# Routing for two heads in one matmul, and score operands padded to 128 rows

## The chip, the cores and the metric

One core of a Trainium2 chip runs the whole program. The metric is device time in microseconds for one launch; runs of the kernel before lie between 767.99 and 769.62 us, with a median of 769.47 us over five. The program alternates between five engines that run side by side, each in the order of its own queue: TensorE (matmuls and transposes), VectorE, ScalarE, GpSimd (called POOL in the profile) and SyncE, which only issues DMAs here.

## The reference

Attention with clusters, then a gated feed-forward layer. There are 4 batches, 8 heads, 768 tokens, 64 dimensions per head and 16 clusters per head. Cut to what matters:

```python
q_assign = argmax(q_n @ c_n.T, axis=-1)        # nearest of 16 centroids, per head
k_assign = argmax(k_n @ c_n.T, axis=-1)
mask   = q_assign[:, None] == k_assign[None, :]
scores = where(mask, q @ k.T / sqrt(64), -1e9)
attn   = softmax(scores)
x      = (attn @ v), heads side by side         # [3072, 512]
out    = (sigmoid(x @ w_gate) * (x @ w_val)) @ w_out   # 512 -> 1536 -> 512
```

The length of a q or k row doesn't change which centroid is the largest, so the kernel normalizes only the centroids.

## The kernel before

The kernel is written with a tile framework that sets the semaphores, hands out the buffers of its pools and fixes the order of each engine's instructions before the run; program order gives the priority, and on the chip each engine works strictly in that fixed order.

The mask is not applied as a mask. For each token a one-hot vector of its cluster is appended below the 64 rows of q and k. The q rows are scaled by 1/8 and their one-hot by 240 (`COH`); the exponential of line 202 has a bias of -240. Where the clusters are equal, 240 is added and taken away again; where they differ, the exponential of about -240 is zero. The augmented operands `q_aug` and `k_aug` have 80 rows (64 + 16), 768 columns, fp16.

The work of one head has three parts.

- Part A, lines 110 to 146: SyncE loads q and k side by side into `qk`, GpSimd loads v into `vv` and appends a column of ones (lines 123, 127). In two halves of 384 tokens, TensorE transposes three 128x128 blocks into `t1` (line 138); ScalarE writes the scaled q into `q_aug` (141), k into `k_aug` (144) and k in float32 into `kT32` (146); VectorE writes q in float32 into `qT32` (145).
- Part B, `phaseB`, lines 147 to 184: for each half of 384 tokens and for q and k apart, a float32 matmul with the head's centroids (64 rows, 16 weight columns) gives 16 scores per token in PSUM (`clq`, line 152; `clk`, line 171; one PSUM buffer each). In the trace each of these routing matmuls is two instructions, called a group below. ScalarE copies the scores to SBUF (160, 179), GpSimd takes the maximum over the 16 partitions (`partition_all_reduce`, 162 and 181), and VectorE compares scores and maximum, which gives the one-hot vectors. For k the comparison writes straight into `k_aug` (184); for q it writes `qoh` (166), and ScalarE scales that by 240 into `q_aug` (167).
- Part C, `phaseC`, lines 186 to 219: in two blocks of 384 queries, for each of six chunks of 128 keys a score matmul `sc` (194), the exponential `es` on ScalarE (202) and an output matmul into `av` (203), 64 rows plus the row of sums from the ones. Then VectorE takes the reciprocal of the sums (211), GpSimd broadcasts it (213) and VectorE multiplies into `xT` (214). `sc` and `av` have two PSUM buffers each, `es` three.

Per batch, part A is written for all eight heads, then B and C with C two heads behind B (lines 221 to 225). The pools keep nine heads of augmented operands and of `qT32` and `kT32`; the small tiles of part B have three buffers for each name. After the fourth batch comes the feed-forward layer (lines 227 to 273) with 128x128 weights and 512 columns per matmul.

Of the kernel before, what the change touches and what calls it, by code (L numbers as in the profile page):

```python
# [8 lines left out]
FP = mybir.dt.float32  # L9
FPR = mybir.dt.float32r  # L10
BF = mybir.dt.bfloat16
HP = mybir.dt.float16
AF = mybir.ActivationFunctionType
ALU = mybir.AluOpType
# [4 lines left out]
def kernel(  # L19
# [11 lines left out]
    nc = tc.nc  # L31
    B, H, S, D = q.shape
    NCL = centroids.shape[1]
# [3 lines left out]
    QB = 384  # L37
    NQB = S // QB
    COH = 240.0
    scale = 1.0 / (D ** 0.5)  # L40

    const = ctx.enter_context(tc.tile_pool(name="const", bufs=1))
    xpool = ctx.enter_context(tc.tile_pool(name="xT", bufs=1))
# [23 lines left out]
        out=wo, in_=moe_w_out.rearrange("(fc p) m -> p fc m", p=128)  # L67
    )

    cT = const.tile([64, H, NCL], FP)  # L70
    with tc.tile_pool(name="cprep", bufs=2) as cp, tc.tile_pool(
        name="cpsum", bufs=2, space=bass.MemoryType.PSUM
    ) as cps:
        for h in range(H):
            cn = cp.tile([NCL, D], FP)
            nc.sync.dma_start(out=cn, in_=centroids[h])
            sq = cp.tile([NCL, D], FP)
            nc.scalar.activation(sq, cn, AF.Square, accum_out=None)
            ss = cp.tile([NCL, 1], FP)
            nc.vector.tensor_reduce(ss, sq, AX.X, ALU.add)  # L80
            nrm = cp.tile([NCL, 1], FP)
            nc.scalar.activation(nrm, ss, AF.Sqrt)
            rn = cp.tile([NCL, 1], FP)
            nc.vector.reciprocal(rn, nrm)
            cnn = cp.tile([NCL, D], FP)
            nc.vector.tensor_scalar(cnn, cn, rn, None, ALU.mult)
            tps = cps.tile([64, NCL], FP)
            nc.tensor.transpose(tps, cnn, ident[:NCL, :NCL])
            nc.scalar.copy(cT[:, h, :], tps)

    with tc.tile_pool(name="qkv", bufs=3) as qkvp, tc.tile_pool(
        name="vvp", bufs=9
    ) as vvp, tc.tile_pool(
        name="aug", bufs=9
    ) as augp, tc.tile_pool(name="esb", bufs=3) as esbp, tc.tile_pool(
        name="p_t1", bufs=2, space=bass.MemoryType.PSUM
    ) as p_t1, tc.tile_pool(
        name="p_cl", bufs=1, space=bass.MemoryType.PSUM
    ) as p_cl, tc.tile_pool(
        name="p_sc", bufs=2, space=bass.MemoryType.PSUM  # L100
    ) as p_sc, tc.tile_pool(
        name="p_av", bufs=2, space=bass.MemoryType.PSUM
    ) as p_av, tc.tile_pool(
        name="small", bufs=3
    ) as smallp, tc.tile_pool(
        name="qt32", bufs=9
    ) as qtp:
        for b in range(B):
            augs = {}
            for h in range(H):  # L110
                dc = h // 2
                r0 = (h % 2) * 64
                qk = qkvp.tile([128, NCH, 2, 64], FP)
                vv = vvp.tile([128, NCH, 65], HP)
                nc.sync.dma_start(
                    out=qk[:, :, 0, :],
                    in_=q[b, h].rearrange("(c p) d -> p c d", p=128),
                )
                nc.sync.dma_start(
                    out=qk[:, :, 1, :],  # L120
                    in_=k[b, h].rearrange("(c p) d -> p c d", p=128),
                )
                nc.gpsimd.dma_start(
                    out=vv[:, :, 0:64],
                    in_=v[b, h].rearrange("(c p) d -> p c d", p=128),
                )
                nc.gpsimd.tensor_copy(vv[:, :, 64:65].rearrange("p c x -> p (c x)"), ones6[:, :NCH])

                q_aug = augp.tile([80, S], HP)
                k_aug = augp.tile([80, S], HP)  # L130
                qT32 = qtp.tile([64, S], FP)
                kT32 = qtp.tile([64, S], FP)
                augs[h] = (q_aug, k_aug, vv, qT32, kT32)

                for g in range(2):
                    t1 = p_t1.tile([128, 3, 128], FP)
                    for cc in range(3):
                        nc.tensor.transpose(t1[:, cc, :], qk[:, g * 3 + cc, :, :], ident)  # L138
                    cols = bass.ts(g, 384)
                    t1f = t1.rearrange("p c x -> p (c x)")  # L140
                    nc.scalar.activation(
                        q_aug[0:64, cols], t1f[0:64, :], AF.Copy, scale=scale
                    )
                    nc.scalar.copy(k_aug[0:64, cols], t1f[64:128, :])  # L144
                    nc.vector.tensor_copy(qT32[:, cols], t1f[0:64, :])  # L145
                    nc.scalar.copy(kT32[:, cols], t1f[64:128, :])  # L146
            def phaseB(h):
                q_aug, k_aug, vv, qT32, kT32 = augs[h]
                for blk in range(2):
                    cols = bass.ts(blk, 384)  # L150
                    clq = p_cl.tile([16, 384], FP)
                    nc.tensor.matmul(  # L152
                        out=clq,
                        lhsT=cT[:, h, :],
                        rhs=qT32[:, cols],
                        start=True,
                        stop=True,
                    )
                    clqs = smallp.tile([16, 384], FP)
                    nc.scalar.copy(clqs, clq)  # L160
                    amq = smallp.tile([16, 384], FP)
                    nc.gpsimd.partition_all_reduce(  # L162
                        amq, clqs, 16, bass_isa.ReduceOp.max
                    )
                    qoh = smallp.tile([16, 384], HP)
                    nc.vector.tensor_tensor(qoh, clqs, amq, ALU.is_equal)  # L166
                    nc.scalar.activation(
                        q_aug[64:80, cols], qoh, AF.Copy, scale=COH
                    )
                    clk = p_cl.tile([16, 384], FP)  # L170
                    nc.tensor.matmul(  # L171
                        out=clk,
                        lhsT=cT[:, h, :],
                        rhs=kT32[:, cols],
                        start=True,
                        stop=True,
                    )
                    clks = smallp.tile([16, 384], FP)
                    nc.scalar.copy(clks, clk)  # L179
                    amk = smallp.tile([16, 384], FP)  # L180
                    nc.gpsimd.partition_all_reduce(  # L181
                        amk, clks, 16, bass_isa.ReduceOp.max
                    )
                    nc.vector.tensor_tensor(k_aug[64:80, cols], clks, amk, ALU.is_equal)  # L184

            def phaseC(h):
                dc = h // 2
                r0 = (h % 2) * 64
                q_aug, k_aug, vv, qT32, kT32 = augs[h]
                for qb in range(NQB):  # L190
                    av = p_av.tile([65, QB], FP)
                    for j in range(NCH):
                        sc = p_sc.tile([128, QB], FP)
                        nc.tensor.matmul(  # L194
                            out=sc,
                            lhsT=k_aug[:, bass.ts(j, 128)],
                            rhs=q_aug[:, bass.ts(qb, QB)],
                            start=True,
                            stop=True,
                        )  # L200
                        es = esbp.tile([128, QB], HP)
                        nc.scalar.activation(es, sc, AF.Exp, bias=nbias)  # L202
                        nc.tensor.matmul(  # L203
                            out=av,
                            lhsT=vv[:, j, :],
                            rhs=es,
                            start=(j == 0),
                            stop=(j == NCH - 1),
                        )
                    rden = smallp.tile([1, QB], FP)  # L210
                    nc.vector.reciprocal(rden, av[64:65, :])  # L211
                    rinv = smallp.tile([64, QB], FP)
                    nc.gpsimd.partition_broadcast(rinv, rden)  # L213
                    nc.vector.tensor_tensor(  # L214
                        xT[r0 : r0 + 64, dc, bass.ds(b * S + qb * QB, QB)],
                        av[0:64, :],
                        rinv,
                        ALU.mult,
                    )

            for i in range(H + 2):
                if i < H:
                    phaseB(i)
                if i >= 2:
                    phaseC(i - 2)

# [2 lines left out]
    if True:  # L229
        with tc.tile_pool(name="h", bufs=2) as hp, tc.tile_pool(  # L230
            name="gs", bufs=3
# [72 lines left out]
```

## Time and profile before

| | |
|---|---|
| median of 5 runs (range) | 769.47 us (767.99 to 769.62) |
| the profiled execution: its time, its span | 767.99 us, 766.2 us |
| TensorE matmuls, busy | 676.0 us, 88% of the span, 2088 instructions |
| TensorE weight loads, beside them | 235.3 us, 31% |
| ScalarE | 451.8 us, 59%, 892 instructions |
| VectorE | 377.2 us, 49%, 416 instructions |
| GpSimd | 265.8 us, 35%, 267 instructions |
| routing matmuls, lines 152 and 171 | 92.1 and 92.4 us busy, 128 instructions each |
| mean granted TensorE clock | 0.759 of full |

Busy times are sums over the whole span, in which the attention and the feed-forward layer have different limits. Matmuls overlap each other, and their ends are modelled, so their rate is read from one start to the next. A releaser behind an arrow is what ended the idle time ahead of an instruction.

### The profile page before, as it was taken

How to read it: one execution, taken by the hardware profiler on the slowest of the kernel's cores; microseconds unless marked ns; L12 is line 12 of the kernel's file. 1: busy time of each engine (PE TensorE's matmuls, PEld its weight loads, DVE VectorE, ACT ScalarE, POOL GpSimd, SP SyncE). 2: the span in 40 equal slices, each digit the busy share in tenths (PEclk: the TensorE clock that was granted, in tenths of full speed). 3: DMA queues.
4: the chain of work that ended last, by engine and by line, in shares of the span. 5: the costliest groups of instructions: out<-in, count | busy, mean ns of one | idle time of the engine just before them, and what ended most of it. 6: DMA issues, size and time to landing. Idle time of an engine off the chain costs nothing.

```text
span 766.2 us, 6830 instructions
## 1 busy us (share of the span) xinstructions
PE 676.0 (88%) x2088; PEld 235.3 (31%) x2088; DVE 377.2 (49%) x416; ACT 451.8 (59%) x892; POOL 265.8 (35%) x267
## 2 busy tenths in 40 slices
PE   0197999897799998789998788999889999999998
PEld 0032222242222223222222321222334444444443
DVE  1144565667446666745666674656755132131221
ACT  2188666788766678776667877666763233232232
POOL 4144555526455542554654255455210000000000
PEclk9999999987555557755555755555559999999999
DMA  7984100124210013230010310000000101101011
GB/s 127 186 125 99 10 5 6 10 28 71 62 26 6 5 10 53 46 83 6 6 11 6 51 42 0 0 1 1 0 1 0 56 3 53 41 15 56 15 41 55
DMA packets 81620, 27.21 MB, mean 36 GB/s; under 512 B 75952, under 2 KB 77488, under 8 KB 81584
## 3 DMA queue, kind: packets, MB, share of 16 engines
q1 hardware_dynamic: 53888, 18.91, 10.1%
q0 software_dynamic: 27696, 7.87, 10.0%
q8 instruction: 16, 0.26, 0.1%
q14 instruction: 20, 0.16, 0.1%
HBM read 28.34 MB, written 6.29 MB: 45 GB/s over the span
## 4 chain that ended last, share of the span: by engine, by line
PE 70%; ACT 12%; issue 8%; POOL 5%; DVE 2%; DMA 2%; ACTq 0%; SPq 0%; POOLq 0%; DVEq 0%
PE av L203 13%; PE sc L194 10%; PE clq L152 10%; PE clk L171 10%; PE gp L241 8%; PE vp L249 8%; PE op L262 8%; ACT es L202 8%; PE t L138 3%; POOL amq L162 2%; POOL amk L181 2%; DMA cn<-in_centroids_dram 1%; ACT k_aug L144 1%; DMA qk<-in_k_dram 1%; ACT kT L146 1%
## 5 line engine op out<-in xcount | busy, mean ns | idle before, releaser
L202 ACT ACTIVATE es<-sc,nbias 128x384 f16<-128x384 f32 x384 | 216.8, 578 | 119.1 <-PE sc L194 104.7
L203 PE MATMUL av<-es,vv 128*65 128x384 f16 x384 | 183.0, 485 | 28.1 <-ACT es L202 12.2
L211 DVE RECIPROCAL rden<-av 1x384 f32<-1x384 f32 x64 | 163.3, 2552 | 56.3 <-PE av L203 55.6
L194 PE MATMUL sc<-q_aug,k_aug 80*128 80x384 f16 x384 | 188.0, 499 | 1.9 <-ACT es L202 0.8
L162 POOL PARTITION_ALL_REDUCE amq<-clqs x64 | 92.4, 1443 | 121.8 <-ACT clqs L160 110.2
L203 PEld LDWEIGHTS <-vv 128*65 128x65 f16 x384 | 58.7, 156 | 170.0 <-issue 152.0
L258 DVE TENSOR_TENSOR hT<-g,vp 128x512 f16<-128x512 f32 x72 | 49.4, 687 | 124.8 <-PE vp L249 124.4
L181 POOL PARTITION_ALL_REDUCE amk<-clks x64 | 100.2, 1566 | 18.3 <-DVE qT L145 8.4
L171 PE MATMUL clk<-kT,cT 64*16 64x384 f32 x128 | 92.4, 823 | 5.0 <-ACT clks L179 5.0
L152 PE MATMUL clq<-qT,cT 64*16 64x384 f32 x128 | 92.1, 821 | 1.8 <-DVE qT L145 1.1
L257 ACT ACTIVATE g<-gp 128x512 f32<-128x512 f32 x72 | 43.0, 597 | 74.8 <-PE gp L241 74.8
L184 DVE TENSOR_TENSOR k_aug<-clks,amk 16x384 f16<-16x384 f32 x64 | 47.5, 742 | 58.5 <-POOL amk L181 58.1
L138 PE MATMUL t<-ident,qk 128*128 128x128 f32 x192 | 54.0, 415 | 23.8 <-ACT kT L146 14.1
L241 PE MATMUL gp<-xT,wg 128*128 128x512 f16 x288 | 74.8, 382 | 0.0
L249 PE MATMUL vp<-xT,wv 128*128 128x512 f16 x288 | 74.3, 381 | 0.0
L194 PEld LDWEIGHTS <-k_aug 80*128 80x128 f16 x384 | 49.9, 130 | 79.1 <-issue 60.8
L213 POOL PARTITION_BROADCAST rinv<-rden x64 | 43.6, 682 | 63.5 <-DVE rden L211 63.5
L166 DVE TENSOR_TENSOR qoh<-clqs,amq 16x384 f16<-16x384 f32 x64 | 43.7, 684 | 43.0 <-POOL amq L162 42.9
L262 PE MATMUL op<-wo,hT 128*128 128x512 f16 x288 | 63.1, 379 | 0.0
L145 DVE COPY qT<-t 64x384 f32<-64x384 f32 x64 | 34.8, 548 | 44.8 <-ACT k_aug L144 43.6
L138 PEld LDWEIGHTS t<-ident,qk 128*128 128x128 f32 x192 | 33.5, 208 | 65.4 <-ACT kT L146 41.7
L214 DVE TENSOR_TENSOR xT<-av,rinv 64x384 f16<-64x384 f32 x64 | 35.2, 550 | 25.9 <-POOL rinv L213 24.7
(37 smaller groups left out, 355.4 us busy)
## 6 DMA issues: line engine op xcount, KB each, us to landing
qk<-in_q_dram SPq DMA_DIRECT2D x32, 192.0 KB, 2.9
qk<-in_k_dram SPq DMA_DIRECT2D x32, 192.0 KB, 3.1
out_dram<-osb SPq DMA_DIRECT2D x24, 256.0 KB, 2.0
vv<-in_v_dram POOLq DMA_DIRECT2D x32, 96.0 KB, 3.5
wg<-in_moe_w_gate_dram POOLq DMA_DIRECT2D x1, 1536.0 KB, 10.8
wv<-in_moe_w_val_dram POOLq DMA_DIRECT2D x1, 1536.0 KB, 10.9
wo<-in_moe_w_out_dram POOLq DMA_DIRECT2D x1, 1536.0 KB, 18.2
cn<-in_centroids_dram SPq DMA_DIRECT2D x8, 4.0 KB, 5.0
```

The costliest lines, as they stand in the source:

```text
L138: nc.tensor.transpose(t1[:, cc, :], qk[:, g * 3 + cc, :, :], ident)
L152: nc.tensor.matmul(out=clq, lhsT=cT[:, h, :], rhs=qT32[:, cols], start=True, stop=True,)
L162: nc.gpsimd.partition_all_reduce(amq, clqs, 16, bass_isa.ReduceOp.max)
L171: nc.tensor.matmul(out=clk, lhsT=cT[:, h, :], rhs=kT32[:, cols], start=True, stop=True,)
L181: nc.gpsimd.partition_all_reduce(amk, clks, 16, bass_isa.ReduceOp.max)
L194: nc.tensor.matmul(out=sc, lhsT=k_aug[:, bass.ts(j, 128)], rhs=q_aug[:, bass.ts(qb, QB)], start=True, stop=True,)
L202: nc.scalar.activation(es, sc, AF.Exp, bias=nbias)
L203: nc.tensor.matmul(out=av, lhsT=vv[:, j, :], rhs=es, start=(j == 0), stop=(j == NCH - 1),)
L211: nc.vector.reciprocal(rden, av[64:65, :])
L241: nc.tensor.matmul(out=gp, lhsT=wg[:, dcc, fc, :], rhs=xT[:, dcc, bass.ts(t, TB)], start=(dcc == 0), stop=(dcc == NDC - 1),)
L249: nc.tensor.matmul(out=vp, lhsT=wv[:, dcc, fc, :], rhs=xT[:, dcc, bass.ts(t, TB)], start=(dcc == 0), stop=(dcc == NDC - 1),)
L262: nc.tensor.matmul(out=op, lhsT=hT[:, fc, bass.ts(tb, 128)], rhs=wo[:, fc, :], start=(fc == 0), stop=(fc == NFC - 1),)
```

## The change

- Routing (part B) works on pairs of heads. Centroids of an even head stand in rows 0 to 63 and columns 0 to 15 of a 128x64 weight, those of the odd head in rows 64 to 127 and columns 32 to 47; the rest is zero. The float32 q and k of two heads stand above each other in one tile `qkT` of 128 rows. One float32 matmul gives the scores of both heads at output partitions 0 to 15 and 32 to 47 of one PSUM tile `cl` (one buffer, for q and k in turn). ScalarE copies the two halves apart; maximum and comparison stay per head.
- The pair's part B stands ahead of the even head's turn in the loop, every second step.
- The scaling moves: q is scaled by 1/128, k by 1/15, the exponential by 240 (1/128 x 1/15 x 240 = 1/8). Both one-hot vectors are then plain ones, the q comparison writes straight into `q_aug`, and the ScalarE instruction of line 167 is gone.
- The augmented operands have 128 rows. Nine pairs of buffers are made once, with rows 64 to 127 set to zero (VectorE for q, GpSimd for k), and are used in turn. The pool of float32 operands has five pair tiles instead of nine single ones of each kind.

```diff
+    ks = 16.0 / COH
+    scale = 1.0 / (16.0 * D ** 0.5)
+    cTp = const.tile([128, H // 2, 64], FP)
+    nc.gpsimd.memset(cTp, 0.0)
...
-            nc.scalar.copy(cT[:, h, :], tps)
+            if h % 2 == 0:
+                nc.scalar.copy(cTp[0:64, h // 2, 0:NCL], tps)
+            else:
+                nc.scalar.copy(cTp[64:128, h // 2, 32 : 32 + NCL], tps)
...
+        for n in range(9):
+            qa_n = augp.tile([128, S], HP, tag=f"qa{n}")
+            ka_n = augp.tile([128, S], HP, tag=f"ka{n}")
+            nc.vector.memset(qa_n[64:128, :], 0.0)
+            nc.gpsimd.memset(ka_n[64:128, :], 0.0)
+            aug_bufs.append((qa_n, ka_n))
...
+                q_aug, k_aug = aug_bufs[(b * H + h) % 9]
+                if h % 2 == 0:
+                    qkT = qtp.tile([128, 2, S], FP)
+                    pairT[h // 2] = qkT
...
-                    nc.scalar.copy(k_aug[0:64, cols], t1f[64:128, :])
-                    nc.vector.tensor_copy(qT32[:, cols], t1f[0:64, :])
-                    nc.scalar.copy(kT32[:, cols], t1f[64:128, :])
+                    nc.scalar.activation(k_aug[0:64, cols], t1f[64:128, :], AF.Copy, scale=ks)
+                    nc.vector.tensor_copy(qkT[r0 : r0 + 64, 0, cols], t1f[0:64, :])
+                    nc.scalar.copy(qkT[r0 : r0 + 64, 1, cols], t1f[64:128, :])
...
+                    for side in range(2):
+                        cl = p_cl.tile([64, 384], FP)
+                        nc.tensor.matmul(
+                            out=cl,
+                            lhsT=cTp[:, pr, :],
+                            rhs=qkT[:, side, cols],
+                            start=True,
+                            stop=True,
+                        )
+                        for g, (qa, ka) in enumerate(
+                            ((q_aug_e, k_aug_e), (q_aug_o, k_aug_o))
+                        ):
+                            r0c = g * 32
+                            clh = smallp.tile([16, 384], FP)
+                            nc.scalar.copy(clh, cl[r0c : r0c + 16, :])
+                            amh = smallp.tile([16, 384], FP)
+                            nc.gpsimd.partition_all_reduce(
+                                amh, clh, 16, bass_isa.ReduceOp.max
+                            )
+                            if side == 0:
+                                nc.vector.tensor_tensor(
+                                    qa[64:80, cols], clh, amh, ALU.is_equal
+                                )
+                            else:
+                                nc.vector.tensor_tensor(
+                                    ka[64:80, cols], clh, amh, ALU.is_equal
+                                )
...
-                        nc.scalar.activation(es, sc, AF.Exp, bias=nbias)
+                        nc.scalar.activation(es, sc, AF.Exp, bias=nbias, scale=COH)
...
-                if i < H:
-                    phaseB(i)
+                if i < H and i % 2 == 0:
+                    phaseB(i // 2)
```

## Rows read from the trace of the kernel before

**Rows 1.** The page's chain that ended last: share by engine, then by line

```profile
PE 70%; ACT 12%; issue 8%; POOL 5%; DVE 2%; DMA 2%; ACTq 0%; SPq 0%; POOLq 0%; DVEq 0%
PE av L203 13%; PE sc L194 10%; PE clq L152 10%; PE clk L171 10%; PE gp L241 8%; PE vp L249 8%; PE op L262 8%; ACT es L202 8%; PE t L138 3%; POOL amq L162 2%; POOL amk L181 2%; DMA cn<-in_centroids_dram 1%; ACT k_aug L144 1%; DMA qk<-in_k_dram 1%; ACT kT L146 1%
```

**Rows 2.** Stretches: length; PE, PEld, DVE, ACT, POOL busy (instructions); clock; DMA; GB/s

```profile
0.00:36.30 36.30, 1.42 (x8) 0.95 (x9) 4.56 (x24) 7.12 (x26) 9.67 (x20) 1.00 1.03 155
83.63:140.77 57.14, 56.42 (x129) 14.36 (x128) 35.44 (x32) 37.17 (x72) 33.23 (x32) 1.00 0.11 7
479.90:538.55 58.65, 57.94 (x131) 14.47 (x131) 35.96 (x33) 37.40 (x74) 31.58 (x26) 0.50 0.00 1
140.77:180.03 39.26, 33.01 (x105) 14.70 (x103) 26.75 (x23) 32.91 (x65) 10.92 (x16) 0.91 0.22 28
36.30:83.63 47.33, 41.59 (x100) 13.68 (x101) 19.48 (x31) 36.84 (x77) 22.82 (x23) 1.00 0.62 101
445.34:479.90 34.56, 29.66 (x65) 7.65 (x64) 18.19 (x25) 25.34 (x54) 20.36 (x15) 0.50 0.11 24
538.55:574.96 36.41, 30.54 (x84) 11.70 (x83) 22.13 (x15) 24.70 (x45) 6.53 (x9) 0.50 0.00 0
574.96:766.20 191.24, 187.66 (x864) 84.60 (x862) 53.02 (x75) 58.31 (x97) 0.67 (x1) 0.99 0.09 34
294.20:297.60 3.40, 3.40 (x14) 2.19 (x13) 2.21 (x1) 2.64 (x5) 0.76 (x1) 0.53 0.80 97
300.00:312.00 12.00, 8.96 (x39) 3.91 (x38) 10.12 (x9) 11.75 (x25) 3.02 (x5) 1.00 0.42 74
```

**Rows 3.** Timeline of TensorE, one steady block: start, duration, engine, line, operation

```profile
104.17 0.52 PE L194 MATMUL sc<-q_aug,k_aug 80*128 80x384 f16 x1
104.49 0.52 PE L203 MATMUL av<-es,vv 128*65 128x384 f16 x1
104.81 0.52 PE L194 MATMUL sc<-q_aug,k_aug 80*128 80x384 f16 x1
105.42 0.48 PE L203 MATMUL av<-es,vv 128*65 128x384 f16 x1
...
106.33 0.52 PE L194 MATMUL sc<-q_aug,k_aug 80*128 80x384 f16 x1
106.79 1.46 PE L152 MATMUL clq<-qT,cT 64*16 64x384 f32 x2
108.18 0.53 PE L203 MATMUL av<-es,vv 128*65 128x384 f16 x1
...
111.31 0.53 PE L194 MATMUL sc<-q_aug,k_aug 80*128 80x384 f16 x1
```

**Rows 4.** The page's 40 slices: granted TensorE clock in tenths

```profile
PEclk9999999987555557755555755555559999999999
```

**Rows 5.** Lines by form: busy us, mean ns of one; idle before, releaser

```profile
L211 DVE RECIPROCAL rden<-av 1x384 f32<-1x384 f32 x64 | 163.3, 2552 | 56.3 <-PE av L203 55.6
L181 POOL PARTITION_ALL_REDUCE amk<-clks x64 | 100.2, 1566 | 18.3 <-DVE qT L145 8.4 <-ACT clks L179 7.9
L138 PEld LDWEIGHTS t<-ident,qk 128*128 128x128 f32 x192 | 33.5, 208 | 65.4 <-ACT kT L146 41.7 <-issue 11.7 <-ACT k_aug L144 6.3
L167 ACT ACTIVATE q_aug<-qoh 16x384 f16<-16x384 f16 x64 | 33.2, 520 | 13.3 <-DVE qoh L166 12.0
L160 ACT COPY clqs<-clq 16x384 f32<-16x384 f32 x64 | 29.3, 458 | 1.4 <-POOL amq L162 0.7
L152 PEld LDWEIGHTS clq<-qT,cT 64*16 64x16 f32 x128 | 8.4, 105 | 38.2 <-ACT clqs L160 27.4 <-issue 6.3 <-DVE qT L145 1.5
masks.py:197 POOL MEMSET ident<- 128x128 f32 x1 | 0.2, 205 | 0.3 <-POOLq L288 0.3
```

**Rows 6.** Timeline of ScalarE in the end stretch: score blocks alone

```profile
550.02 1.22 ACT L202 ACTIVATE es<-sc,nbias 128x384 f16<-128x384 f32 x2 [0.47 <-PE sc L194]
551.55 1.22 ACT L202 ACTIVATE es<-sc,nbias 128x384 f16<-128x384 f32 x2 [0.31 <-PE sc L194]
```

More of the change, by code (lines that the diff above doesn't have):

```diff
@@ L39 @@
     COH = 240.0
-    scale = 1.0 / (D ** 0.5)
+    ks = 16.0 / COH
+    scale = 1.0 / (16.0 * D ** 0.5)
     const = ctx.enter_context(tc.tile_pool(name="const", bufs=1))
@@ L68 @@
     )
-    cT = const.tile([64, H, NCL], FP)
+    cTp = const.tile([128, H // 2, 64], FP)
+    nc.gpsimd.memset(cTp, 0.0)
     with tc.tile_pool(name="cprep", bufs=2) as cp, tc.tile_pool(
@@ L93 @@
     ) as vvp, tc.tile_pool(
-        name="aug", bufs=9
+        name="aug", bufs=1
     ) as augp, tc.tile_pool(name="esb", bufs=3) as esbp, tc.tile_pool(
@@ L105 @@
     ) as smallp, tc.tile_pool(
-        name="qt32", bufs=9
+        name="qt32", bufs=5
     ) as qtp:
+        aug_bufs = []
+        for n in range(9):
[4 more added lines that the diff above has]
+            aug_bufs.append((qa_n, ka_n))
         for b in range(B):
             augs = {}
+            pairT = {}
             for h in range(H):
@@ L127 @@
                 nc.gpsimd.tensor_copy(vv[:, :, 64:65].rearrange("p c x -> p (c x)"), ones6[:, :NCH])
[L129 to L133, printed above, removed]
+                q_aug, k_aug = aug_bufs[(b * H + h) % 9]
[3 more added lines that the diff above has]
+                else:
+                    qkT = pairT[h // 2]
+                augs[h] = (q_aug, k_aug, vv)
                 for g in range(2):
@@ L143 @@
                     )
-                    nc.scalar.copy(k_aug[0:64, cols], t1f[64:128, :])
-                    nc.vector.tensor_copy(qT32[:, cols], t1f[0:64, :])
-                    nc.scalar.copy(kT32[:, cols], t1f[64:128, :])
-            def phaseB(h):
-                q_aug, k_aug, vv, qT32, kT32 = augs[h]
+                    nc.scalar.activation(k_aug[0:64, cols], t1f[64:128, :], AF.Copy, scale=ks)
+                    nc.vector.tensor_copy(qkT[r0 : r0 + 64, 0, cols], t1f[0:64, :])
+                    nc.scalar.copy(qkT[r0 : r0 + 64, 1, cols], t1f[64:128, :])
@@ L149, in phaseB @@
+            def phaseB(pr):
+                qkT = pairT[pr]
+                q_aug_e, k_aug_e, _ = augs[2 * pr]
+                q_aug_o, k_aug_o, _ = augs[2 * pr + 1]
                 for blk in range(2):
                     cols = bass.ts(blk, 384)
[L151 to L183, printed above, removed]
@@ L184, in phaseB @@
-                    nc.vector.tensor_tensor(k_aug[64:80, cols], clks, amk, ALU.is_equal)
+                    for side in range(2):
[21 more added lines that the diff above has]
+                                )
+                            else:
+                                nc.vector.tensor_tensor(
+                                    ka[64:80, cols], clh, amh, ALU.is_equal
+                                )
@@ L188, in phaseC @@
                 r0 = (h % 2) * 64
-                q_aug, k_aug, vv, qT32, kT32 = augs[h]
+                q_aug, k_aug, vv = augs[h]
                 for qb in range(NQB):
```

## Prediction

> **What bounds the kernel now.** I read the views from the whole to one repeated block. The chain that ended last is 70% TensorE and 12% ScalarE, and the routing matmuls `clq` and `clk` (lines 152 and 171) hold 10% of the span each [rows 1]. So TensorE first, but stage by stage: I cut the span at the starts of the reciprocal of line 211, which runs once per block (half a head in `phaseC`, six score tiles). That gives four kinds of stretch per batch, times below from [rows 2]:
>
> - steady: blocks at a constant pitch, eight of them from 83.63 to 140.77 us, again four times, 57 to 59 us each. TensorE is busy 56.4 of 57.1 us, ScalarE 37.2, VectorE 35.4, GpSimd 33.2. TensorE sets the pace.
> - turn: the last blocks of a batch beside the transposes of the next, 39.3 us. ScalarE is busy 32.9, TensorE 33.0: mixed, ScalarE slightly the tighter.
> - opening: rest of the transposes and the first heads' routing, 47.3 us for the first batch, about 35 for the other three (34.6 for the last): TensorE 29.7, ScalarE 25.3.
> - end: score blocks alone, 36.4 us; then the FFN, 191.2 us, which the change doesn't touch. Ahead of all this 36.3 us pass in which no attention matmul runs.
>
> One steady block in order of time [rows 3]: from the score matmul at 104.17 to the same one a block later at 111.31 are 7.14 us. A score or output matmul takes the 0.32 us from 104.17 to 104.49; twelve make 3.84. The `clq` group starts at 106.79 and the next instruction at 108.18, 1.39 us; ahead of it the score matmul that started at 106.33 held 0.46 instead of 0.32. So one routing group costs 1.39 + 0.14 = 1.53, two cost 3.06, and 7.14 - 3.84 - 3.06 = 0.24 is left: one wait for an exponential (0.61 instead of 0.32 between 104.81 and 105.42).
>
> The clock: the slices show the lower level, 1.2 GHz, in most of the attention and the upper, 2.4 GHz, in the FFN [rows 4]. The 1.00 of the first steady stretch is only what was recorded before the first change: its blocks have the length of those marked 0.50 in the last [rows 2]. I take 1.2 GHz for all steady stretches.
>
> **The change, part by part.**
>
> *Routing matmuls.* 128 groups (32 heads, two column blocks, q and k) become 64, each for two heads, with 128 rows and 64 weight columns in place of 64 and 16. The output still has 384 columns. Is a fuller group as quick? A score matmul with 80 rows and an output matmul with 128 both take 0.32 [rows 3], so rows cost nothing; I take 1.53 per group. Weight loads: 105 ns with 16 float32 columns, 208 ns with 128 [rows 5]. Were 64 columns as slow as 128, and both loads of a group in the open, 64 groups would lose 64 x 2 x 0.103 = 13 us; hidden, nothing. Only the first load of a group shows now (the 0.14), and 64 columns lie 48/112 of the way from 16 to 128, so I take 64 x 0.044 = 3 us.
>
> *What that frees in the steady stretches.* Four stretches of eight blocks are 32 blocks; each has one q and one k group [rows 3], so 32 groups go here. A removed group frees 1.53, but it also covered exponential latency. Without any routing two tiles have a pitch of 551.55 - 550.02 = 1.53 against 4 x 0.32 = 1.28 of matmul, a stall of 0.25 [rows 6]. A new block is three such pairs and one group, which covers one stall: 3 x 1.53 + 1.53 - 0.25 = 5.87, a gain of 7.14 - 5.87 = 1.27. Bounds: 1.53 if the remaining waits stay as now, 1.0 if the second stall and a copy's delay come on top. 32 x 1.27 = 41 us (32 to 49).
>
> *Who covers the new pace.* Per steady block the other engines are busy an eighth of the first stretch [rows 2]. ScalarE: 37.17 / 8 = 4.65, less the scaling of line 167 that goes (0.52 [rows 5]): 4.1; the routing copies stay 128, two heads' halves being copied apart. VectorE: 35.44 / 8 = 4.4, with a reciprocal of 2.55 in it; q's comparison now writes at row 64 as k's does, which I take to be as long. GpSimd: 33.23 / 8 = 4.2, its all-reduces being as many as before. All lie under 5.87, so none is late next, but VectorE has only 1.4 us of air.
>
> *Openings and turns.* About 32 of the removed groups lie here. Were TensorE the limit throughout: 32 x 1.39 = 44 us. Were ScalarE: its removed scalings, 32 x 0.52 = 17 us. Were it the chain copy, all-reduce, comparison, whose number of all-reduces is unchanged: nothing. TensorE is busy 86% of the opening and ScalarE 73% [rows 2], neither fills it, so I take half of the upper bound, 22 us (0 to 44). Pairing holds the routing of an even head until the odd head's transposes are done; the next batch's transposes already run in the turn, so I charge nothing. If that cover goes, the wait is one head's six ScalarE copies, at about the 0.46 of a routing copy [rows 5] 2.8 us, four times 11 us, within these bounds.
>
> *Augmented operands with 128 rows.* Scores contract 128 rows in place of 80: same 0.32. Nine pairs of buffers cleared once: the one clearing in the trace took 0.205 us for 128 columns [rows 5], six times that for 768 is an estimate of 1.2 us, nine on VectorE and nine on GpSimd about 11 us each. Both are idle most of the first 36.3 us (VectorE busy 4.6, GpSimd 9.7 [rows 2]), and the zeroed rows are needed by the first score matmul, long after. Cost nothing; 11 us if GpSimd's queue then holds up the first v loads and the routing behind them.
>
> *Moved scales, buffers.* A scale inside a ScalarE copy or exponential adds no instruction; I cost it at nothing (line 141 has one already, and the exponential a bias). The number of augmented buffers is nine as before; five pair tiles stand for nine single ones. One PSUM tile `cl` serves q and k in place of one each, and one ring of three `clh` in place of two rings of three. That is where a new wait can come from (below).
>
> Sum: -41 - 22 + 3 = -60 us. The profiled execution took 767.99 us (span 766.2); the median of the five runs is 769.47, so 709.5, called 709.
>
> *A rule weighed against this.* The Trainium skill, "TensorEngine Tiling (Array Packing)", section PSUM Bottleneck, warns that packing speeds up TensorE but not the emptying of PSUM, which can become the limit. It speaks against this change: half the matmuls, the same 128 copies. The steady stretch gives ScalarE 4.1 of the new 5.87 us, so by the rows TensorE stays the limit and the sum stands. By the rule ScalarE would be the block, 4.1 us, and the sum 32 x 1.77 = 57 us lower; it could come to that only with a quicker TensorE, the first rival.
>
> **Rivals.**
>
> *The clock rises.* In a turn, with transposes of 128 rows and columns between scores and outputs, the clock stood at a mean of 0.53 from 294.2 to 297.6 us and at 1.00 from 300 to 312, though TensorE was busy only 9.0 of those 12 us; in the steady stretches, busy 99% with groups of 64 rows and 16 columns, it stays at the lower level [rows 2, 4]. The changed kernel has scores of 128 rows and routing of 128 rows by 64 columns in that place. For: what runs there is fuller, more like the turn and the FFN. Against: the output matmul keeps its 65 columns, and in the end stretch score and output alone stay at 0.50. The block is then bound by the in-order chains of ScalarE and VectorE, 4.1 and 4.4 of work, with 0.5 of waits 4.9: 32 x (5.87 - 4.9) = 31 us more in the steady stretches, and an eighth of each opening, four times 4 us: 709 - 47 = 662. The Trainium skill, "TensorE: Matmul & The Clock Gate", section Part 1, has activity release the clock. By that alone the steady stretches before would stand at the upper level already and there would be nothing to rise; the trace disagrees (0.50 at 99% busy).
>
> *A smaller gain.* All-reduces, whose number is unchanged, hold the openings, and steady blocks gain only 1.0: 769.5 - 32 + 3 = 740. For: in an opening all of the first heads' all-reduces, 1.57 each [rows 5], must end before the first block can. Against: GpSimd is busy only 20.4 of 34.6 us there [rows 2].
>
> *Slower: ScalarE is held by the shared ring.* A copy into `clh` waits until the comparison three copies earlier has freed its slot, and that one waits for its all-reduce and, on VectorE, for a 2.55 us reciprocal in front of it. ScalarE works in order, so the exponentials behind stand, and with them scores and outputs; with a single `cl` the next routing group stands too. If each of 64 groups exposes one all-reduce, 64 x 1.57 = 100 us: 769.5 - 60 + 100 = 810. It decides from 60 / 64 = 0.94 us per group on. For: half the slots. Against: all-reduces come at 2 per block, 3.1 of 5.87 us, so a slot is nearly always free in time.
>
> That the change doesn't do what it says is not likely: the groups are written out one by one.
>
> **How the numbers follow.** Forecast 709, chance 0.50, own range 690 to 728 (the bounds of steady and opening, not both at their ends). Clock 662, 0.27. Smaller gain 740, 0.13. Slower 810, 0.10. The range 655 to 746 leaves out the slower case and some of the faster ones. Differences under 0.2% can't be told here: faster 0.89, same 0.01, slower 0.10.
>
> **What would show it.** Right: 128 routing instructions in place of 256 (two per group, [rows 3]); steady pitch 5.7 to 6.1; the clock at 0.50 there; ScalarE busy some 70% of a block; no line-167 successor. The clock case: marks of 1.00 in steady stretches, score matmuls 0.16 apart. The slower case: exponentials idle behind a `clh` copy that waits for a comparison. The prediction is wrong if the steady pitch stays above 6.6 or falls under 5.3.

## The result: 666 us, at the place of the first rival

The changed kernel takes 665.96 us (median of nine runs, 664.67 to 669.16) against 769.34 for the one before: a ratio of 0.8666, 95% interval 0.865 to 0.8682. The forecast of 709 was 43 us too slow. The rival in which the clock rises had given 662. One run of the pairing-alone kernel below took 1495 us, more than twice its others, and no figure in the text uses it.

The page of the changed kernel, its slices and the chain that ended last:

```profile
span 664.1 us, 6557 instructions
PE   0046767875777685777676677766799999999997
PEclk9999797799689898699988679878799999999999
PE 39%; POOL 18%; DVE 15%; ACT 13%; issue 10%; DMA 5%; POOLq 0%; ACTq 0%; SPq 0%; DVEq 0%
```

TensorE's share of the chain fell from 70% to 39% [rows 1]; GpSimd and VectorE, 7% together before, hold 33%. In most of the attention the clock marks are 6 to 9 where [rows 4] has 5 to 7. After the first change of level on record, the attention before had 369 us at the lower level and 44 at the upper; now it has 113 and 297 (sums over the record of clock changes, up to the rise at the FFN; the record begins at 164 us of the span before and at 65 us now).

The stretches, cut as before at the starts of the reciprocal (length; TensorE, its weight loads, VectorE, ScalarE, GpSimd busy; clock; DMA): four steady ones of eight blocks, then a turn, two openings, the end, and the rest to the last instruction.

```profile
80.44:126.54 46.10, 32.30 (x115) 11.89 (x115) 40.62 (x38) 36.24 (x75) 38.10 (x36) 0.89 0.14 9
183.21:223.59 40.38, 29.31 (x113) 11.00 (x113) 37.80 (x35) 34.10 (x70) 34.39 (x34) 0.96 0.16 10
288.71:327.01 38.30, 26.96 (x108) 10.25 (x107) 35.29 (x32) 32.29 (x66) 32.74 (x32) 1.00 0.16 11
392.59:430.38 37.79, 27.76 (x106) 10.33 (x105) 34.63 (x32) 30.24 (x61) 28.89 (x24) 0.95 0.00 0
...
327.01:359.50 32.49, 23.26 (x100) 10.62 (x99) 25.23 (x22) 27.75 (x57) 7.70 (x13) 0.95 0.31 46
...
36.30:80.44 44.14, 28.36 (x87) 13.38 (x88) 16.95 (x28) 35.03 (x72) 20.38 (x20) 0.92 0.64 109
157.85:183.21 25.36, 17.14 (x55) 6.51 (x56) 18.14 (x23) 20.54 (x44) 21.26 (x17) 0.80 0.34 67
...
430.38:467.64 37.26, 25.00 (x83) 9.72 (x81) 22.27 (x16) 21.93 (x41) 5.21 (x8) 0.82 0.00 1
467.64:664.10 196.46, 188.04 (x864) 84.81 (x864) 52.56 (x74) 58.31 (x97) 0.67 (x1) 0.98 0.09 33
```

Against [rows 2], all stretches of a kind added up:

| | before | after | difference | forecast |
|---|---|---|---|---|
| steady, 4 x 8 blocks | 231.6 | 162.6 | -69 | -41, +3 for weight loads |
| turns, 3 | 117.6 | 96.4 | -21 | 0 |
| openings, 4 | 153.1 | 135.1 | -18 | -22 |
| end | 36.4 | 37.3 | +1 | 0 |
| FFN, from the last reciprocal on | 191.2 | 196.5 | +5 | 0 |

The sum is -102, the difference of the spans. The steady pitch is 38.30 / 8 = 4.79 us in the third stretch, where VectorE is busy 92%, and 4.7 to 5.8 over the four; before it was 7.14. The cuts lie at the reciprocals of VectorE, so work of other engines can move from one kind of stretch to another when the order changes.

One steady block on TensorE (start, duration, what; in brackets its idle time and what ended it):

```profile
303.67 0.32 PE L213 MATMUL av<-es,vv 128*65 128x384 f16 x1
303.83 0.32 PE L204 MATMUL sc<-qa_n,ka_n 128*128 128x384 f16 x1
304.00 0.32 PE L213 MATMUL av<-es,vv 128*65 128x384 f16 x1
...
306.19 0.32 PE L213 MATMUL av<-es,vv 128*65 128x384 f16 x1 [0.35 <-ACT es L212]
307.30 0.86 PE L170 MATMUL cl<-qkT,cTp 128*64 128x384 f32 x2 [0.16 <-ACT clh L182]
308.62 0.35 PE L213 MATMUL av<-es,vv 128*65 128x384 f16 x1 [0.46 <-DVE xT L224]
```

From 303.67 to 303.83 are 0.16 us where [rows 3] had 0.32: the upper level, 2.4 GHz. TensorE now waits for all three others: for an exponential, for a routing copy, and, at the start of a block, for the multiply of an earlier block that frees the output's PSUM buffer.

### The profile page after: what moved, and what is told of

The parts are those of the page before. It is cut to its first block, busy times and chain, and to the rows that moved or that the text cites. A ratio compares the mean times of both kernels' runs of the same rounds, so it can differ in the third digit from the quotient of the medians.

```text
span 664.1 us, 6557 instructions
## 1 busy us (share of the span) xinstructions
PE 495.0 (75%) x1960; PEld 208.4 (31%) x1960; DVE 386.0 (58%) x425; ACT 411.8 (62%) x828; POOL 273.3 (41%) x277
## 4 chain that ended last, share of the span: by engine, by line
PE 39%; POOL 18%; DVE 15%; ACT 13%; issue 10%; DMA 5%; POOLq 0%; ACTq 0%; SPq 0%; DVEq 0%
POOL amh L184 14%; PE gp L251 10%; PE vp L259 9%; PE op L272 9%; DVE rden L221 8%; ACT es L212 7%; PE av L213 4%; POOL rinv L223 3%; DMA vv<-in_v_dram 2%; PE sc L204 2%; PE cl L170 2%; ACT qkT L161 2%; DVE qa_n L188 2%; DVE ka_n L192 2%; DVE xT L224 2%
## 5 line engine op out<-in xcount | busy, mean ns | idle before, releaser
L184 POOL PARTITION_ALL_REDUCE amh<-clh x128 | 183.8, 1474 | 46.5 <-ACT clh L182 33.8
L213 PE MATMUL av<-es,vv 128*65 128x384 f16 x384 | 131.7, 359 | 68.5 <-ACT es L212 44.9
L204 PE MATMUL sc<-qa_n,ka_n 128*128 128x384 f16 x384 | 132.5, 349 | 8.8 <-ACT es L212 4.7
L170 PE MATMUL cl<-qkT,cTp 128*64 128x384 f32 x128 | 70.6, 641 | 22.6 <-ACT clh L182 21.3
L204 PEld LDWEIGHTS <-ka_n 128*128 128x128 f16 x384 | 39.4, 103 | 109.4 <-issue 98.9
L182 ACT COPY clh<-cl 16x384 f32<-16x384 f32 x128 | 59.5, 465 | 22.5 <-PE cl L170 9.1
L188 DVE TENSOR_TENSOR qa_n<-clh,amh 16x384 f16<-16x384 f32 x64 | 49.2, 783 | 19.7 <-POOL amh L184 18.9
L192 DVE TENSOR_TENSOR ka_n<-clh,amh 16x384 f16<-16x384 f32 x64 | 48.4, 769 | 19.9 <-POOL amh L184 19.4
L160 DVE COPY qkT<-t 64x384 f32<-64x384 f32 x64 | 34.8, 548 | 28.8 <-ACT ka_n L159 28.1
L224 DVE TENSOR_TENSOR xT<-av,rinv 64x384 f16<-64x384 f32 x64 | 35.2, 550 | 26.5 <-POOL rinv L223 25.6
L153 PEld LDWEIGHTS t<-ident,qk 128*128 128x128 f32 x192 | 28.8, 185 | 68.6 <-ACT qkT L161 49.2
L280 ACT COPY osb<-op 128x512 f32<-128x512 f32 x24 | 14.0, 585 | 53.5 <-PE op L272 53.5
## 6 DMA issues: line engine op xcount, KB each, us to landing
wv<-in_moe_w_val_dram POOLq DMA_DIRECT2D x1, 1536.0 KB, 10.6
```

What stands on the lines that cost most here:

```text
L170: nc.tensor.matmul(out=cl, lhsT=cTp[:, pr, :], rhs=qkT[:, side, cols], start=True, stop=True,)
L184: nc.gpsimd.partition_all_reduce(amh, clh, 16, bass_isa.ReduceOp.max)
L188: nc.vector.tensor_tensor(qa[64:80, cols], clh, amh, ALU.is_equal)
L204: nc.tensor.matmul(out=sc, lhsT=k_aug[:, bass.ts(j, 128)], rhs=q_aug[:, bass.ts(qb, QB)], start=True, stop=True,)
L213: nc.tensor.matmul(out=av, lhsT=vv[:, j, :], rhs=es, start=(j == 0), stop=(j == NCH - 1),)
```

## The experiments

Theory F: the 128 rows of the score matmuls raised the clock. Theory R: the routing matmuls did, either as they are fuller or as they are half as many. Times below are medians; ratios are to the kernel before, with 95% intervals.

**Pairing alone.**

```diff
-                            lhsT=k_aug[:, bass.ts(j, 128)],
-                            rhs=q_aug[:, bass.ts(qb, QB)],
+                            lhsT=k_aug[0:80, bass.ts(j, 128)],
+                            rhs=q_aug[0:80, bass.ts(qb, QB)],
```

> The changed kernel, its score matmuls reading only rows 0 to 79 of the padded operands; paired routing stays. Theory F (the 128 rows of the score matmuls are what raised the clock): steady stretches back at 0.50, block pitch 5.7 to 6.1, 700 to 715 us, which is also what the predicted sum gives without a clock change. Theory R (the fuller, rarer routing matmuls raised it): clock in the steady stretches as in the changed kernel, 0.87 to 1.00, 663 to 669 us. Both together needed: in between, the clock changing back and forth, 675 to 700 us.

682 us (three runs of 679 to 684 and the profiled one below, 685.5), ratio 0.8862 (0.8813 to 0.8912): in between, as written for "both together". Its profile was taken from one more run of the same kernel:

> The kernel of e1_rows80 once more, for a profile. If its time of about 682 us comes from a clock that is at the upper level in most of the steady stretches (theory R), their pitch is 4.6 to 5.2 and the clock there 0.8 to 1.0; if it comes at the lower level, pitch 5.6 to 6.

685.5 us. The clock in its 40 slices:

```profile
PEclk9998778698799697579759577555599999999999
```

and one of its steady stretches of eight blocks:

```profile
295.47:334.29 38.82, 29.81 (x107) 11.16 (x107) 35.54 (x33) 32.77 (x66) 32.74 (x32) 0.88 0.17 11
```

The clock goes back and forth: 232 us at the lower level, 208 at the upper. Where it is high (0.88) the pitch is 38.82 / 8 = 4.85, as in the changed kernel; the other three stretches, at 0.66 to 0.92, have 5.1 to 6.0. Neither theory alone.

**Padding alone**, in the kernel before.

```diff
-                q_aug = augp.tile([80, S], HP)
-                k_aug = augp.tile([80, S], HP)
+                q_aug, k_aug = aug_bufs[(b * H + h) % 9]   # nine pairs, [128, S], rows 64 to 127 zeroed once
```

> The kernel before with nothing changed but the padding: score operands of 128 rows, rows 80 to 127 zero, 256 routing instructions as before. Theory F: steady stretches mostly at 1.00, a routing group about 0.75 us, block pitch 4.9 to 5.3 set by VectorE and ScalarE, 670 to 695 us. Theory R: clock 0.50, pitch 7.14 as before, 767 to 773 us.

Four runs took 725 to 741 us, ratio 0.9601 (0.9533 to 0.967). Zero rows that add nothing to any result are worth about 4%. It missed both expectations: the clock rose, but only in parts.

The clock in its slices, then a part of its third steady stretch and four blocks of its last:

```profile
PEclk9999999995575678555576865899889999999999
```

```profile
327.00:365.00 38.00, 37.55 (x86) 9.45 (x86) 23.34 (x22) 24.70 (x48) 21.80 (x23) 0.50 0.12 8
464.89:485.01 20.12, 15.42 (x64) 4.88 (x64) 18.97 (x16) 17.60 (x38) 13.69 (x12) 1.00 0.01 1
```

From 327 to 365 us it runs as the kernel before did, 0.50 with TensorE busy 99%, pitch 7.14; in its last steady stretch blocks take 20.12 / 4 = 5.03 us at 1.00, with TensorE busy 77%. The same kind of block ran at either level within one execution, so what the matmuls fill does not decide alone. What else does stays open.

**Fill or number of the routing matmuls?** Two kernels fill the other corners of a square. In both cuts a call stands on one line.

```diff
                         nc.tensor.matmul(out=cl, lhsT=cTp[:, pr, :], rhs=qkT[:, side, cols], start=True, stop=True)
+                        nc.tensor.matmul(out=cl, lhsT=cTp[:, pr, :], rhs=qkT[:, side, cols], start=True, stop=True)
```

> The kernel of e1_rows80 (80 score rows, paired routing) with each routing matmul issued twice into the same output: 128 groups as in the kernel before, but each of 128 rows and 64 columns. If what the routing matmuls fill raised the clock: steady stretches mostly at 1.00, pitch 4.8 to 5.6, 680 to 705 us. If their being half as many raised it: steady at 0.50, pitch about 7.1, 735 to 770 us.

675 us, ratio 0.8768 (0.8737 to 0.8798), below both ranges: with twice the routing matmuls it is quicker than without, 682. The lower level falls from 232 to 123 us, and the steady stretches stand at 0.88 to 0.96. But their pitch is 5.9 to 6.3, not 4.8 to 5.6: the four steady stretches grew from 169.8 to 196.2 us and the four openings fell from 137.9 to 103.6. The planned order changed too, so the 7 us are not the clock's alone.

```diff
-                    nc.tensor.matmul(out=clk, lhsT=cT[:, h, :], rhs=kT32[:, cols], start=True, stop=True)
-                    nc.scalar.copy(clks, clk)
+                    nc.scalar.copy(clks, clq)
```

> The kernel before without the routing matmuls of k: k's scores are copied from q's PSUM tile, so the k clusters are wrong and the rest of the work is all there. 64 groups of 64 rows and 16 columns. If the number of groups raised the clock: steady mostly at 1.00, pitch 4.8 to 5.3, 680 to 700 us. If what they fill did: steady at 0.50, pitch 5.6 to 6.1, 705 to 730 us, which would also be the price of the halving at a constant clock.

723.9 us, ratio 0.9406 (0.9383 to 0.943), where the expectation for "what they fill" stood. Six steady blocks of it:

```profile
216.45:252.21 35.76, 33.12 (x83) 9.94 (x81) 26.16 (x25) 28.99 (x57) 25.08 (x25) 0.50 0.13 9
```

The clock stays at 0.50 and a block takes 35.76 / 6 = 5.96, near the 5.87 that the prediction worked out for a constant clock. The first blocks after an opening take longer; over all eight the pitch of a stretch is 6.1 to 6.5. The square, with 80 score rows:

| routing matmuls | 64 rows x 16 columns | 128 rows x 64 columns |
|---|---|---|
| 128 groups | 769 (before) | 675 |
| 64 groups | 724 | 682 |

The right-hand column also has the other edits of the pairing (no line-167 scaling, one ring). Those don't explain why twice the matmuls is not slower there and 45 us slower on the left. The marks say it more directly: 64 thin groups leave the steady stretches at 0.50, 64 full ones have them at 0.66 to 0.92, 128 full ones at 0.88 to 0.96. What the routing matmuls fill raised the clock, not their smaller number. Whether it is their rows (64 to 128) or their columns (16 to 64) was not separated. With 128 score rows the lower right corner is 666, the upper left 725 to 741, the upper right 658 (below).

**Wider output matmul.**

```diff
-                    av = p_av.tile([65, QB], FP)
+                    av = p_av.tile([128, QB], FP)      # vv 128 wide, columns 65 to 127 zero
...
```

> The changed kernel with the output matmul's weights widened from 65 to 128 columns (zeros; the results of rows 65 to 127 are not used). If what each matmul fills decides the clock, the pieces at 0.50 that the changed kernel still has in openings and at the end go to 1.00 and the time falls by 3 to 12 us, 654 to 663. If columns make no difference: 664 to 669 us, clock mean 0.91 as now.

670.5 us, ratio 0.8719 (0.8684 to 0.8754), mean clock 0.90: no gain, if anything 4 us lost. Zero columns of the output matmul brought no gain, unlike the zero rows of the scores.

**Is there more in the clock?** The changed kernel with its routing matmuls issued twice, as above:

> The changed kernel with each routing matmul issued twice into the same output, so TensorE does 64 groups of unused work. If the pieces at the lower clock still cost time, as between e1_rows80 and e5_twice (682 to 675 us): faster than the changed kernel, 655 to 664 us, mean clock above 0.92. If the clock has given all that it can: the 64 groups of 0.65 us lie beside other work or on the path, 666 to 690 us.

658.4 us, ratio 0.8565 (0.8528 to 0.8602), 8 us faster than the changed kernel; the lower level falls from 113 to 41 us.

```profile
PEclk9998799999899999998999999887799999999999
```

That unused matmuls pay for themselves by the clock is not shown, though. The added instructions also change the planned order, and the gain doesn't lie in the steady blocks: the four steady stretches grew from 162.6 to 191.6 us, with some 83 of the 128 all-reduces in them instead of 70, and the four openings fell from 135.1 to 100.9. What the clock gave of the 8 us isn't separated.

**What bounds a block at the upper level.** First VectorE, then the ring, one at a time:

```diff
-                    nc.vector.reciprocal(rden, av[64:65, :])
+                    nc.vector.tensor_copy(rden, av[64:65, :])
```

> The changed kernel with a copy in place of the reciprocal (so the outputs are not normalized): VectorE loses 64 x 2.0 us. If VectorE is what bounds a block at the upper clock (busy 92% there): pitch from 4.8 to 4.2 to 4.5, bound then by ScalarE, 635 to 655 us. If the all-reduce chain or ScalarE bounds it: 660 to 666 us.

664.2 us, ratio 0.8636 (0.8614 to 0.8657): 128 us less VectorE work (64 x 2.0) bought some 2 us, no more than the runs spread. VectorE alone, busy 92%, did not hold the whole; what a quicker reciprocal does at the old order isn't shown, for the order changed: blocks near the openings became longer (6.5 us), and routing copies waited 35 us for comparisons instead of 10.6.

```diff
-        name="p_cl", bufs=1, space=bass.MemoryType.PSUM
+        name="p_cl", bufs=2, space=bass.MemoryType.PSUM
...
-                            clh = smallp.tile([16, 384], FP)
+                            clh = smallp.tile([16, 384], FP, bufs=8)     # amh likewise
```

> The changed kernel with two PSUM buffers for cl and eight slots instead of three for clh and amh. If the shared ring and the single cl hold ScalarE and TensorE (waits of copies on comparisons 10.6 us, of routing on copies 21.3 us in the changed kernel's trace): 645 to 658 us. If VectorE, busy 92% of a steady stretch, is the bound: 662 to 667 us.

668.7 us, ratio 0.8695 (0.8659 to 0.8731): nothing gained, though the waits shrank. The copies' group in the changed kernel and, below it, in this one (busy, mean ns; idle before and releasers):

```profile
L182 ACT COPY clh<-cl 16x384 f32<-16x384 f32 x128 | 59.5, 465 | 22.5 <-PE cl L170 9.1 <-DVE qa_n L188 8.4 <-DVE ka_n L192 2.2
L224 DVE TENSOR_TENSOR xT<-av,rinv 64x384 f16<-64x384 f32 x64 | 35.2, 550 | 26.5 <-POOL rinv L223 25.6
```

```profile
L182 ACT COPY clh<-cl 16x384 f32<-16x384 f32 x128 | 59.5, 465 | 4.3 <-PE cl L170 1.5 <-DVE qa_n L188 0.5
L224 DVE TENSOR_TENSOR xT<-av,rinv 64x384 f16<-64x384 f32 x64 | 35.2, 550 | 50.9 <-POOL rinv L223 50.4
```

The copies' wait fell from 22.5 to 4.3 us, and the multiply's wait for GpSimd's broadcast doubled (25.6 to 50.4): the wait moved. So the broadcast next:

```diff
+            nc.vector.memset(vv_n, 1.0)                    # vv 128 wide, columns 64 to 127 ones
...
-                    nc.vector.reciprocal(rden, av[64:65, :])
-                    nc.gpsimd.partition_broadcast(rinv, rden)
+                    nc.vector.reciprocal(rinv, av[64:128, :])
```

> The changed kernel with 64 columns of ones instead of one beside v, so the output matmul leaves the sums on 64 partitions; the reciprocal takes all 64 and GpSimd's broadcast goes. If a block is held by the chain reciprocal, broadcast, multiply that frees the output's PSUM buffer (waits of the output matmul on it 17.7 us, of the multiply on the broadcast 25.6 us in the changed kernel): 640 to 655 us. If it is held by the all-reduce chain: GpSimd loses 0.79 per block, 645 to 660 us. If ScalarE holds it: 662 to 667 us.

658.0 us, ratio 0.8558 (0.8528 to 0.8589): 8 us faster, a little short of the 640 to 655 written for the chain of the broadcast. The gain lies in the end stretch, 28.8 us in place of 37.3, and not in the steady blocks (161.8 against 162.6). The end of the changed kernel has an output matmul standing for the multiply, and below it is the end of this one:

```profile
443.83 1.74 PE L213 MATMUL av<-es,vv 128*65 128x384 f16 x4 [1.54 <-DVE xT L224]
430.70:459.50 28.80, 21.04 (x75) 7.52 (x73) 22.78 (x16) 20.08 (x38) 1.56 (x2) 0.82 0.00 1
```

The last all-reduces end 1.6 us into this stretch, so what held its blocks was the chain of reciprocal, broadcast and multiply; the copy in place of the reciprocal had shortened it too, to 25.5 us. In the steady blocks that chain was not the bound by itself. And both together:

> The kernel of e8_ones64 with two PSUM buffers for cl and eight slots for clh and amh. If the ring is what is late next once the broadcast is gone: 5 to 15 us under e8_ones64; if not: within 3 us of it.

639.0 us, ratio 0.8325 (0.8288 to 0.8361), the fastest kernel here, 4% under the changed one. The wider ring with the second `cl` (not separated) is worth 19 us once the broadcast is gone, more than the 5 to 15 expected, and nothing before. The 19 us lie in the steady stretches: 140.6 us in place of 161.8, a pitch of 4.4. In this kernel the reciprocal, the copies and one steady stretch stand as

```profile
L225 DVE RECIPROCAL rinv<-av 64x384 f32<-64x384 f32 x64 | 163.6, 2558 | 27.7 <-PE av L217 26.4
L186 ACT COPY clh<-cl 16x384 f32<-16x384 f32 x128 | 59.5, 465 | 5.4 <-PE cl L174 3.3
186.56:221.88 35.32, 26.70 (x109) 9.52 (x108) 34.44 (x32) 33.13 (x68) 24.29 (x19) 1.00 0.19 14
```

VectorE is now busy 34.44 of 35.32 us, 98%, so a steady block here has little to gain from anything else.

Last, this kernel with its routing matmuls issued twice:

> The kernel of e9_ones64_rings with each routing matmul issued twice. If the lower-clock pieces still cost what they did in the changed kernel (658 against 666 us): 628 to 635 us, mean clock above 0.95. If in this kernel ScalarE is the bound at either clock: 636 to 645 us.

652.3 us, ratio 0.849 (0.8466 to 0.8514): 13 us slower, with the mean clock up from about 0.93 to 0.95. Missed: the higher clock repaid nothing here. The steady stretches grew from 140.6 to 166.1 us; whether by TensorE's extra work or by the new order isn't separated.

## Why the prediction was right and wrong

- *TensorE bounds the steady block, and a routing group costs 1.53 us.* Right in the main: with half the groups at the lower clock (the kernel of 64 thin groups) settled blocks had a pitch of 5.96 against 5.87 forecast, and 45 us went in all. Of these 29 lay in the steady stretches, where 41 were forecast, 15 in the openings and 9 in the turns. The pairing without the rise of the clock wasn't run.
- *"I take 1.2 GHz for all steady stretches."* Right for the kernel before, and carried over to the changed one, where it failed: of the 43 us that the forecast was off, 28 lie in the steady stretches, which stood at 0.89 to 1.00. By its own sign (a steady pitch under 5.3) it was wrong in three of the four stretches. The forecast's steady term was -41; measured, -69. That 666 lies in the range of 655 to 746 is owed to the clock rival, given 0.27, and not to the forecast.
- *How near the rival came.* Its steady term, -41 - 31 = -72, was within 3 us, and its pitch of 4.9 became 4.7 to 5.8. The rest is luck: its openings, -22 - 16 = -38, were 20 us too much, and it had nothing for the turns, which gave 21. Its reason for the pitch, the work of VectorE and ScalarE with 0.5 of waits, isn't shown either: the kernel with the quicker reciprocal had no shorter steady stretches (197.2 us), and those of the fastest kernel shrank when waits between engines went.
- *What raised the clock.* The rival named scores of 128 rows and routing of 128 by 64. Both count: padding alone about 4%, pairing alone 11%, together 13%; of the 11%, halving thin groups at the lower clock gave 6%. The reasons given against it were no obstacle: the output matmul kept its 65 columns, 128 brought nothing (670 us), and the end stretch, at 0.50 before, has 0.82.
- *The turns.* Forecast: nothing. Measured: -21, at clocks of 0.90 to 0.95 in place of 0.67 to 0.91. A mixed stretch was booked as ScalarE's because ScalarE was "slightly the tighter"; TensorE busy 33.0 of 39.3 us was the sign that it too had something to give. The 64 thin groups, with the steady stretches at 0.50, gave 9 of it; what the clock gave of the rest is not measured apart.
- *The openings.* -18 against -22: near, but by luck, as the term was half of an upper bound; the 64 thin groups gave -15.
- *The shared ring.* The slower rival was wrong as the bound of the whole, and its wait was there: copies waited 10.6 us for comparisons, where it had priced 100, and ring and second `cl` together were worth 19 us when the broadcast was gone.
- *Weight loads.* 160 ns for 64 columns measured, 149 interpolated. *Clearing.* 0.74 us each on GpSimd and 0.38 on VectorE, where the estimate was 1.2; the first transposes, which waited for a k load, started at 37.45 us instead of 36.30, so at most 1.1 us of it showed.
- *Missed altogether:* the FFN's first matmul stood 4.1 us for the last multiply, which it hadn't before. With two buffers for `cl`, which fill PSUM in the attention as before, that wait is 0.0. That points to the PSUM buffer that the FFN's first tile gets; it was not isolated further. The FFN's row in the table grew by 5 us.

The lines behind the weight loads, the clearing and the FFN's wait, from the changed kernel:

```profile
L170 PEld LDWEIGHTS cl<-qkT,cTp 128*64 128x64 f32 x128 | 14.5, 160 | 51.4 <-ACT clh L182 47.2 <-issue 2.3 <-ACT es L212 1.9
L118 POOL MEMSET ka_n<- 64x768 f16 x9 | 6.2, 737 | 0.1
L117 DVE MEMSET qa_n<- 64x384 uint32 x9 | 3.4, 378 | 1.4 <-PEq L298 0.9
L251 PE MATMUL gp<-xT,wg 128*128 128x512 f16 x288 | 74.8, 382 | 4.1 <-DVE xT L224 4.1
```

## What to carry to other kernels

Where TensorE is busy all the time and its marks still show the lower clock, ask what its matmuls fill before counting what they cost: zero rows alone gave about 4% here, and 64 full routing groups ran in 682 us, 128 in 675, where 64 thin ones took 724. Weigh such a rival by how much of the path stands on the clock, not as a side case. When removing one wait gains nothing, look which wait grew by as much: here two edits gave 0 and 8 us alone and 27 together. And compare the stretches as well as the total: an added instruction can change the planned order and move time from one kind of stretch to another, as the doubled routing did.

## What the runs showed of the hardware that was not expected

- With 80 score rows, the attention stood on record at the upper level for 307 us with 128 full routing groups, for 208 with 64 full ones and for 48 with 64 thin ones. With thin groups the steady stretches were at the lower level though TensorE was busy 92 to 99% of them.
- Zero rows count: padding the scores from 80 to 128 rows alone raised the time at the upper level from 44 to 205 us. The same blocks ran at either level within that execution.
- A float32 reciprocal of 384 elements per partition took 2.55 us on one partition and 2.56 on 64.
